# Thresholded attention with a SwiGLU layer: half-size input pieces, four chunks turned on TensorE, six weights buffers

## The chip, the cores and the metric

The kernel runs on one core of one Trainium2 chip. The metric is device time in microseconds, the median over several executions. Before the change it is 536.67 us over 4 runs (535.39 to 538.34). The profiled execution took 535.39 us, of which the span from its first to its last instruction is 533.6 us.

A core has five engines with queues of their own. TensorE (PE) multiplies matrices and writes to PSUM, VectorE (DVE) and ScalarE (ACT) work through rows, GpSimd (POOL) does the same on SBUF alone, and SyncE (SP) issues DMAs. Each queue runs in the order in which it was built; an instruction that waits holds back all that is behind it.

## The reference

q, k and v are [8 batches, 8 heads, 576 rows, 64] in float32. The attention keeps, in each row, only scores within tau = 0.02 of the row's maximum; the result goes through an RMS norm and a SwiGLU layer with 512 inputs and 1536 hidden units.

```python
scores = scale * np.matmul(q, k.transpose(0, 1, 3, 2))
thresh = np.max(scores, axis=-1, keepdims=True) - tau
scores = np.where(scores >= thresh, scores, -1000000000.0)
...
attn = np.exp(scores)
attn = attn / (np.sum(attn, axis=-1, keepdims=True) + 1e-09)
return np.matmul(attn, v)
...
xn = x / rms * rms_g
g = xn @ w_gate
silu = g * (1.0 / (1.0 + np.exp(-g)))
return (silu * (xn @ w_val)) @ w_out
```

## The kernel before

The 4608 output rows are worked on as 36 chunks of 128 rows. A batch has 576 rows, which is four chunks and a half; the halves of two batches make one chunk of its own ("v"), the others are "m". A chunk has four steps, one for each pair of heads, so there are 144 steps. A step is one row of scores for two heads:

- **Scores** (L690): TensorE multiplies q and k in float32 in two halves of PSUM, `s_ps`. The first 32 steps are made one at a time, the rest in bursts of 1024 columns, 1.78 steps each (L736).
- **Minima** (L723): VectorE writes -score/8 to `ssb` and keeps the row minimum `mx`. The second operand, which is added, is a row of zeros, `zrow` (L185).
- **Threshold and exponential**: GpSimd adds tau (L764), ScalarE masks with two Prelu operations (L775) and writes the exponential to one of three `wsb` buffers (L782).
- **Turning the weights**: for the first 16 steps TensorE transposes them (L827) and VectorE copies the result out (L836); from step 16 on, one DMA transpose for each step, issued by SP (L842), writes one of five `wt` buffers (NWT, L219).
- **Values product** (L860, L865): one for two steps, then VectorE divides by the sums (L882, L883).

After a chunk's four steps, `emit_x` squares the rows on ScalarE (L900), finds and applies the norm on GpSimd (L903 to L908) and turns the 128x512 rows `xn` into `xnT` by another DMA transpose on SP (L912). With `N_XPE` above 0 the first chunks would be turned by TensorE instead (L918 to L931); it is 0. Two or four chunks make a group for the **FFN**: 12 slices, each with a gate product (L966), a value product (L971), tanh on ScalarE, two VectorE operations (L983, L988), and then the output products (L1037, or L1012 for the last group).

**Inputs.** Batches 0 and 1 have loads of their own. From batch 2 on (`BLOCKED`), `emit_block_loads` brings the q and the k of two pairs of heads by one 576 KB DMA each (L369), GpSimd swaps 32-row blocks (L383) and VectorE turns 32x32 blocks (`emit_blocks`, L397 to L406). Values come in two 512 KB DMAs for each batch (L602), one for each half of the partitions, and GpSimd casts them for each pair of heads (L579). SP issues all of these loads, the transposes and the output stores through one queue.

**The order.** Nothing is ordered by hand. Every operation has a priority in steps, a modelled duration and what it depends on; `order_ops` (L56) plays them through and writes each engine's queue. `RANK` (L26) adds an offset for each kind of operation. For a DMA the planner adds an allowance until it has landed: `LAT_TR` for transposes, `LAT_QB`, `LAT_V` for the loads. A load is also tied to the score burst of the step that its priority names (`gated`, L249). So a changed allowance or rank moves instructions on all engines.

Of the kernel before, what the change touches and what calls it, by code (L numbers as in the profile page):

```python
# [25 lines left out]
RANK = dict(  # L26
    ACT={"emit_ffn/ev": 400, "emit_ffn/store": 40, "emit_ffn/tanh": -350, "emit_k_tail/ev": -230, "emit_q_tail/ev": -70, "emit_qk/ev": 390,
        "emit_softmax/prelu": 170, "emit_x/sq": -320},
    DVE={"emit_av/half": -39, "emit_blocks/turn_k": 90, "emit_blocks/turn_kt": 140, "emit_blocks/turn_q": 280, "emit_burst/ttr": -50, "emit_ffn/ev":
        185, "emit_ffn/gate": -20, "emit_ffn/silu": -44, "emit_k_tail/ev": -110, "emit_qk/ev": -120, "emit_softmax/ev": 250},  # L30
    PE={"emit_av/fn": -340, "emit_burst/fn": -110, "emit_ffn/gmm": 21, "emit_ffn/omm": 22, "emit_ffn/vmm": -20, "emit_k_tail/tr": 220,
        "emit_q_tail/tr": -70, "emit_softmax/tr": -110},
    POOL={"emit_block_loads/swap": 60, "emit_softmax/nthr": -240, "emit_x/mean": -110, "emit_x/norm": -50, "round_/<lambda>": 60, "main/<lambda>":
        760, "main/cast": -300},
)
# [114 lines left out]
def kernel(  # L150
# [12 lines left out]
    nc = tc.nc  # L163
# [20 lines left out]
    id16 = sb("id16", [128, 128], FP16)  # L184
    zrow = sb("zrow", [128, S], FP16)  # L185
    mhalf = sb("mhalf", [128, 1])
# [29 lines left out]
    esb = [sb(f"esb{i}", [128, S], FP16) for i in range(NES if set(WAYS) != {"pp"} else 0)]  # L216
    NW = 3
    wsb = [sb(f"wsb{i}", [128, 2, S], FP16) for i in range(NW)]
    NWT = 5  # L219
    wt = [sb(f"wt{i}", [128, 9, 128], FP16) for i in range(NWT)]  # L220
# [66 lines left out]
    def setup():  # L287
        o_id = add("POOL", 2000.0, -100, [], lambda o: make_identity(nc, id32))
        o_z = add("DVE", 350.0, -200, [], lambda o: nc.vector.memset(zrow, 0.0))

        def warm(o):

            for _ in range(WARM):
                nc.tensor.matmul(s_ps[0][:, 0:512], zrow[:, 0:128], zrow[:, 0:512], start=True, stop=True)

        o_w = add("PE", WARM * 380.0, -200, [o_z], warm)

        def consts(o):
            nc.vector.tensor_copy(out=id16, in_=id32)
            nc.vector.memset(mhalf, -0.5)  # L300

        def vconst(o):
            for i in range(2):
                nc.vector.memset(va[i][:, :, :, D:D + 1], 1.0)
                nc.vector.memset(va[i][64:128, :, 8], 0.0)
                nc.vector.memset(va[i][0:64, :, 9], 0.0)

        o_c = add("DVE", 300.0, -100, [o_id, o_z], consts)
        o_v = add("DVE", 2000.0, -90, [], vconst)
        o_g = add("SP", 350.0, -0.5, [], lambda o: nc.sync.dma_start(  # L310
            out=rmsg, in_=moe_rms_g.rearrange("(c p) -> p c", p=128)), dma=100.0)
        return o_id, o_c, o_v, o_g
# [46 lines left out]

    def emit_block_loads(b, g, prio):  # L360

        done = {}
        for j, src in ((1, k), (0, q)):
            before = turned[g, j] if (g, j) in turned else [x for t in tr_of for x in t[-NQK:]] + (tail_load["use", 0] if g else [])
            own = nat[:, g, 1 - j]

            def load(o, src=src, own=own):
                a0 = 2 * GROUP * g
                nc.sync.dma_start(out=own.rearrange("p a r d -> p a (r d)"),  # L369
                                  in_=src[b, a0:a0 + 2 * GROUP].rearrange("(a h) (m r) d -> h m a (r d)", h=2, r=RUN))  # L370

            pr = prio + BLOCK_STEP * (1 - j)
            lo = gated(add("SP", COST["sp_qb"], pr, before, load, dma=DMA_NS["qkb"], bulk=True), pr)
            lo.lat = LAT_QB
            done[j] = []
            for h in range(2):
                lower, upper = slice(64 * h, 64 * h + 32), slice(64 * h + 32, 64 * h + 64)
                moves = [(spare[upper], own[lower, :, :, 32:64]), (own[lower, :, :, 32:64], own[upper, :, :, 0:32]),
                         (own[upper, :, :, 0:32], spare[upper])]
                last = [lo] + spare_use[-1:]  # L380
                for dst, at in moves:
                    def swap(o, dst=dst, at=at):
                        nc.gpsimd.tensor_copy(out=dst, in_=at)  # L383

                    last = [add("POOL", COST["swap"], prio + SWAP_AT, last, swap)]
                spare_use.append(last[0])
                done[j] += last
            turned[g, j] = []
        return done

    def emit_blocks(b, p, prio, los):
# [18 lines left out]
        tq = gated(add("DVE", COST["turn_q"], prio, los[0] + free, turn_q), prio)  # L410
        turned[g, 0].append(tq)
        turned[g, 1] += [tk, tt]
        for c in range(4):
# [157 lines left out]
    def emit_v(b, prio):  # L571
# [13 lines left out]
        for p in range(NP):  # L585
# [12 lines left out]
            if b >= BLOCKED and p == 0:  # L598
                lo = []
                for g in range(2):  # L600
                    def load_block(o, g=g):
                        nc.sync.dma_start(out=vst8[64 * g:64 * g + 64].rearrange("m h (c d) -> m h c d", d=D),  # L602
                                          in_=v[b].rearrange("h (m r) d -> m h r d", r=RUN)[:, :, 4 * g:4 * g + 4])

                    pl = pr + V_FROM + V_STEP * g
                    lo.append(gated(add("SP", COST["sp_v"], pl, v_cast[-NP:], load_block, dma=2 * DMA_NS['v'], bulk=True), pl))
                    lo[-1].lat = LAT_V
            ca = add("POOL", COST["cast_v"], (pr + V_CAST if b >= BLOCKED else pr + 1 if b else p - 1.0), lo + free(p), round_(
                t[:, p, 0:8, 0:D].rearrange("q (c h) d -> q h c d", h=2),
# [18 lines left out]
    def emit_batch_inputs(b):  # L628
        base = first_step[b - 1] if b else -10
        if b == 1:  # L630
            base += B1_BASE
        if b < BLOCKED:
            emit_tail_load(b, base + (4 if b else 1))
        if b == 0:
            q0_use.extend(emit_first())
        else:
            for p in range(NP):
                pr = base + 3.3 * p + 3
                if b >= BLOCKED:
                    los = los if p % GROUP else emit_block_loads(b, p // GROUP, pr - 3)  # L640
                    emit_blocks(b, p, pr, los)
                else:
                    emit_qk(b, p, pr)
                if p == 0 and b < BLOCKED:
                    emit_k_tail(b, pr + 2)
        emit_v(b, base + 5 if b else -1)
        if b % 2 and b < BLOCKED:
            emit_q_tail(b // 2, v_step[b // 2] - 1.5)
# [27 lines left out]
    def emit_burst(segs, prio, runs):  # L676
# [35 lines left out]
        for s, lo, hi, at in segs:  # L712
# [7 lines left out]
            for h in range(2):  # L720
                def ttr(o, s=s, lo=lo, hi=hi, at=at, h=h, first=first, last=last):
                    m = s % 6
                    nc.vector.tensor_tensor_reduce(  # L723
                        out=ssb_of(s)[:, h, lo:hi], in0=s_ps[h][:, at:at + hi - lo], in1=zrow[:, lo:hi],
                        scale=-1.0 / 8.0, scalar=3.0e38 if first else mxp[m][:, h:h + 1], op0=ALU.add, op1=ALU.min,
# [33 lines left out]
    def emit_softmax(s):  # L759
# [80 lines left out]
        else:  # L840
# [5 lines left out]
            w_ready[s] = [t]  # L846

    def emit_av(s):

# [4 lines left out]
        def fn(o):  # L854
            for i in range(2):
# [14 lines left out]
        deps = w_ready[s - 1] + w_ready[s] + [x for bb in bs for i in range(2) for x in v_ready[bb, p1 - i]]  # L870
        o = add("PE", 2 * COST["av_main" if kind == "m" else "av_virt"], s + AV_PRIO, deps, fn, ring="R",
                mode=0 if kind == "m" else 3)
# [7 lines left out]
        def half(_):  # L880
# [5 lines left out]

        half_ev.append(add("DVE", COST["rz"] + COST["xmul"], s + HALF_PRIO, [o] + x_done.get(ci - 2, []), half,
                           frees=(o, 0)))

    def emit_x(ci, s, slot, off):  # L890
# [22 lines left out]

        a = add("DVE" if on_dve else "ACT", 660.0 if on_dve else COST["sq"], s + 1.5, half_ev[-2:] + xn_of[ci - 2:ci - 1], sq)
        bb = add("POOL", COST["pool_mean"], s, [a, o_c], mean)
        c = add("POOL", COST["xn"], s - 1, [bb], norm)
        x_done[ci] = [c]
        if ci < N_XPE:  # L918
# [4 lines left out]

            p_ = add("PE", 240.0, s, [c, o_c], trp, ring="R")
            xn_of.append(p_)
# [4 lines left out]

            return add("DVE", COST["evac_w"] + 50.0, s, [p_] + xnT_use.get(slot, []), ev, frees=(p_, 0))  # L931
        t = add("SP", COST["sp_tr"], s, [c] + xnT_use.get(slot, []), tr, dma=DMA_NS['xt'])
# [256 lines left out]
LAG = 8.0  # L1189
LAT_TR = 2500.0  # L1190
LAT_LD = 2000.0
# [18 lines left out]
WAYS = ("pp",)  # L1210
NSTAGE = 3
NQK = 3
BLOCKED = 2
BLOCK_STEP = 3.0
SWAP_AT = 4.0
V_STEP = 1.0
V_FROM = 6.0
V_CAST = 9.0
LAT_QB = 4500.0
LAT_V = 4000.0  # L1220
LAT_W = 3000.0
W_FROM = 2.0
W_STEP = 0.4
N_XPE = 0
N_PE = 16
# [40 lines left out]
```

## Time and profile before

| | |
|---|---|
| median of 4 runs | 536.67 us |
| profiled execution | 535.39 us |
| its span | 533.6 us |
| TensorE busy | 520.7 us |
| VectorE busy | 465.1 us |
| ScalarE busy | 444.0 us |
| GpSimd busy | 223.9 us |
| moved by DMA | 89.03 MB |

In the profile a busy share is the time in which at least one instruction of the engine runs. Matmuls overlap each other, and their ends are modelled. A row of the table of stretches reads: stretch, its length, the busy time (and instructions) of PE, PEld (the loading of the stationary operand, which overlaps PE), DVE, ACT and POOL, the granted TensorE clock, the mean busy share of the DMA engines, GB/s. A row of waits reads: who waited, for whom, microseconds in all, how often, the longest. A row of the timeline or the chain begins with its start and its length in microseconds. SPq is SP's issuing of a DMA. A DMA's "landing" runs from its issue to the arrival of its data, so the chain's DMA pieces are longer than SP's part of them.

The last score burst starts at about 455 us. Until then all parts run side by side; after it only the rest of the FFN is left, with TensorE busy for the whole of 460 to 520 us.

### The profile page before, as it was taken

Reading aid. Unit: us, or ns where it says so; the run is one execution under the profiler, and the core shown is the slowest. Engines: PE = TensorE matmul, PEld = TensorE weight load, DVE = VectorE, ACT = ScalarE, POOL = GpSimd, SP = SyncE. Lnnn points to the kernel's source line nnn. Section 1 sums busy time; section 2 is a strip of 40 time slices with the busy share of each in tenths; the row PEclk is TensorE's granted clock in tenths of the full one; section 3 lists DMA queues with packets and bytes.
Section 4 is the critical chain, followed back from the end, with each engine's and each line's share of the span. In section 5 each row is a group of like instructions: output and inputs, shape, how many; then the busy total and the mean of one; then the engine's idle time right before and its main releaser. Section 6 shows DMA issues by size and latency. Waiting matters only on the chain.

```text
span 533.6 us, 14315 instructions
## 1 busy us (share of the span) xinstructions
PE 520.7 (98%) x5352; PEld 273.7 (51%) x5352; DVE 465.1 (87%) x1342; ACT 444.0 (83%) x648; POOL 223.9 (42%) x478
## 2 busy tenths in 40 slices
PE   8999999999999999999999999999999999999995
PEld 4766676554645454445454454545454545444442
DVE  4998999978999999999999899989999888765641
ACT  5999999888997999889989999899999999831210
POOL 2368756615653157545743456445732022110000
PEclk9999999999999999999999999999999999999998
DMA  9999999959998789999997899999996768631103
GB/s 203 234 298 307 193 200 187 211 84 227 202 178 142 165 162 176 200 200 183 192 180 153 168 192 207 186 211 175 210 165 120 143 119 118 137 66 30 30 22 98
DMA packets 220486, 89.03 MB, mean 167 GB/s; under 512 B 196864, under 2 KB 206592, under 8 KB 220416
## 3 DMA queue, kind: packets, MB, share of 16 engines
q1 hardware_dynamic: 217616, 86.02, 81.7%
q0 software_dynamic: 1600, 1.57, 1.9%
q8 instruction: 42, 0.69, 0.6%
q10 hardware_dynamic: 1200, 0.52, 0.4%
q14 instruction: 28, 0.23, 0.1%
HBM read 37.75 MB, written 9.44 MB: 88 GB/s over the span
## 4 chain that ended last, share of the span: by engine, by line
PE 66%; DVE 15%; DMA 7%; ACT 6%; issue 3%; POOL 1%; SPq 1%; DVEq 0%; ACTq 0%; POOLq 0%
PE s_ps L690 20%; PE ring L966 12%; PE ring L971 12%; PE ring L1037 11%; DVE ssb L723 8%; DMA wt<-wsb 4%; PE ring L865 4%; ACT ssb L775 3%; DMA xnT<-xn 2%; PE s_ps L1012 2%; DVE sl L983 2%; ACT wsb L782 2%; PE ring L860 1%; DVE hf L988 1%; DVE stg L988 1%
## 5 line engine op out<-in xcount | busy, mean ns | idle before, releaser
L775 ACT ACTIVATE ssb<-ssb,nth 128x576 f32<-128x576 f32 x288 | 209.8, 766 | 16.6 <-POOL nth L764 15.8
L723 DVE CUSTOM_DVE_ANT_0 ssb<-s_ps,zrow 128x576 f32<-128x576 f32 (+8 forms) x288 | 169.3, 635 | 8.9 <-PE s_ps L690 6.8
L690 PE MATMUL s_ps<-qkt 64*64 64x288 f32 (+9 forms) x2256 | 171.2, 411 | 1.5 <-DVE mx L723 0.8
L782 ACT ACTIVATE wsb<-ssb 128x1152 f16<-128x1152 f32 x144 | 166.8, 1159 | 4.2 <-DMA wt<-wsb 1.9
L690 PEld LDWEIGHTS s_ps<-qkt 64*64 64x64 f32 (+1 forms) x2256 | 81.2, 134 | 67.4 <-issue 25.9
L966 PE MATMUL ring<-xnT,wg 128*128 128x512 f16 (+1 forms) x456 | 107.1, 357 | 2.0 <-DMA xnT<-xn 1.5
L971 PE MATMUL ring<-xnT,wv 128*128 128x512 f16 (+1 forms) x456 | 107.0, 357 | 0.1
L980 ACT ACTIVATE th<-ring 128x512 f32<-128x512 f32 (+1 forms) x114 | 61.6, 541 | 39.2 <-PE ring L966 38.8
L764 POOL TENSOR_SCALAR nth<-mx 128x2 f32<-128x2 f32 x144 | 30.8, 214 | 148.4 <-DVE mx L723 141.8
L983 DVE SCALAR_TENSOR_TENSOR sl<-th,ring 128x512 f32<-128x512 f32 (+1 forms) x114 | 70.7, 622 | 9.5 <-ACT th L980 9.4
L966 PEld LDWEIGHTS <-wg 128*128 128x128 f16 x480 | 43.3, 98 | 53.2 <-issue 15.3
L971 PEld LDWEIGHTS <-wv 128*128 128x128 f16 x480 | 44.1, 98 | 48.2 <-issue 9.0
L723 DVE CUSTOM_DVE_ANT_0 ssb<-s_ps,zrow,mxp 128x128 f32<-128x128 f32 (+7 forms) x112 | 52.9, 509 | 15.6 <-PE s_ps L690 13.1
L865 PE MATMUL ring<-va,wt 128*128 128x65 f16 (+1 forms) x1280 | 51.7, 193 | 0.0
L865 PEld LDWEIGHTS <-wt 128*128 128x128 f16 (+1 forms) x1280 | 46.3, 100 | 4.3
L1037 PE MATMUL ring<-wo,hf 128*128 128x512 f16 x204 | 48.0, 379 | 0.0
L988 DVE TENSOR_TENSOR stg<-ring,sl 128x512 f16<-128x512 f32 (+1 forms) x59 | 36.7, 627 | 2.2
L1037 PE MATMUL ring<-wo,stg 128*128 128x512 f16 x156 | 36.8, 379 | 0.0
L988 DVE TENSOR_TENSOR hf<-ring,sl 128x512 f16<-128x512 f32 (+1 forms) x55 | 34.0, 623 | 1.6
L903 POOL TENSOR_SCALAR irm<-ssq 128x1 f32<-128x1 f32 x36 | 6.9, 190 | 66.4 <-ACT xn L900 65.6
L383 POOL COPY spare<-qkx 32x576 f32<-32x576 f32 x48 | 31.6, 658 | 7.1 <-DMA qkx<-in_k_dram 2.8
L860 PE MATMUL ring<-va,wt 128*128 128x130 f16 (+1 forms) x160 | 32.3, 225 | 1.4 <-DMA wt<-wsb 1.4
(71 smaller groups left out, 495.0 us busy)
## 6 DMA issues: line engine op xcount, KB each, us to landing
qkx<-in_k_dram SPq DMA_DIRECT2D x12, 576.0 KB, 4.7
qkx<-in_q_dram SPq DMA_DIRECT2D x12, 576.0 KB, 4.7
out_dram<-osb SPq DMA_DIRECT2D x51, 128.0 KB, 2.6
vst<-in_v_dram SPq DMA_DIRECT2D x12, 512.0 KB, 5.5
stg<-in_moe_w_gate_dram SPq DMA_DIRECT2D x6, 512.0 KB, 5.8
stg<-in_moe_w_val_dram SPq DMA_DIRECT2D x6, 512.0 KB, 6.1
vst<-in_v_dram SPq DMA_DIRECT2D x8, 256.0 KB, 4.3
wt<-wsb SPq DMA_TRANSPOSE x128, 3.7
```

Of the source, the lines that this page charges most:

```text
L690: nc.tensor.matmul(s_ps[h][rows, at:at + hi - lo], lhs(hs), k_of(bb, p, h)[hs, lo:hi], start=True, stop=True)
L723: nc.vector.tensor_tensor_reduce(out=ssb_of(s)[:, h, lo:hi], in0=s_ps[h][:, at:at + hi - lo], in1=zrow[:, lo:hi], scale=-1.0 / 8.0, scalar ...
L775: nc.scalar.activation(out=sb_[:, h], in_=sb_[:, h], func=PRELU, scale=-1.0, bias=nth[m][:, h:h + 1], **PRELU_KW)
L782: nc.scalar.activation(out=wsb[s % NW], in_=sb_, func=AF.Exp)
L860: nc.tensor.matmul(ring[o.slot[0]][rs, at:at + 2 * (D + 1)], w[:, 4, rs], va[vi][:, p, 8:10].rearrange("p e d -> p (e d)"), start=True, st ...
L865: nc.tensor.matmul(ring[o.slot[0]][rs, at:at + D + 1], w[:, 5 * h + j, rs], va[vi][:, p, 2 * j + h], start=False, stop=(h == 1 and j == 3))
L966: nc.tensor.matmul(ring[o.slot[0]][:, 0:n], wg[d][:, fs], xnT[slot][:, d, 0:n], start=(d == 0), stop=(d == 3))
L971: nc.tensor.matmul(ring[o.slot[0]][:, 0:n], wv[d][:, fs], xnT[slot][:, d, 0:n], start=(d == 0), stop=(d == 3))
L980: nc.scalar.activation(out=th[i][:, 0:n], in_=ring[g.slot[0]][:, 0:n], func=AF.Tanh, scale=0.5)
L983: nc.vector.scalar_tensor_tensor(out=sl[i][:, 0:n], in0=th[i][:, 0:n], scalar=1.0, in1=ring[g.slot[0]][:, 0:n], op0=ALU.add, op1=ALU.mult)
L988: nc.vector.tensor_tensor(out=hf[hi][:, 0:n], in0=ring[vv.slot[0]][:, 0:n], in1=sl[i][:, 0:n], op=ALU.mult)
L1037: nc.tensor.matmul(ring[(first or o).slot[0]], hf[hs[fc][0]][:, 128 * j:128 * (j + 1)], wo[:, fc], start=(fc == 0), stop=(fc == NFC - 1))
```

## The change

It has five parts.

1. The 576 KB loads of q and k become two of 288 KB, each for one pair of heads, at 1.25-step distances (`LOAD_STEP`) from the beginning of the batch before; a piece waits for the turns of its own pair only. The two 512 KB values loads become four of 256 KB for half of the heads each (`V_PARTS`), and a cast waits for the two pieces of its own heads. The planner's allowances for them go down by 500 ns.
2. `N_XPE` = 4: the rows of the first four chunks are turned by four 128x128 TensorE transposes and one VectorE copy.
3. Six `wt` buffers instead of five, and `LAT_TR` goes from 2500 to 3000 ns. To make room, the row of zeros gives way to a single column that is broadcast; the warm-up matmuls read the first `xn` buffer, cleared for that.
4. Other ranks in all four tables.
5. `soon`, an offset for the first chunks, is added to some priorities. It is set to 0 and does nothing.

```diff
-    PE={"emit_av/fn": -340, "emit_burst/fn": -110, "emit_ffn/gmm": 21, "emit_ffn/omm": 22, "emit_ffn/vmm": -20, "emit_k_tail/tr": 220,
-        "emit_q_tail/tr": -70, "emit_softmax/tr": -110},
+    PE={"emit_av/fn": -370, "emit_burst/fn": 16, "emit_ffn/gmm": 20, "emit_ffn/omm": 23, "emit_ffn/vmm": -40, "emit_k_tail/tr": 210, "emit_q_tail/tr":
+        -160, "emit_qk/tr": 60, "emit_softmax/tr": -40, "emit_x/trp": 20},
...
-    zrow = sb("zrow", [128, S], FP16)
+    zcol = sb("zcol", [128, 1], FP16)
...
-    NWT = 5
+    NWT = N_WT
...
+        def zero(o):
+            nc.vector.memset(zcol, 0.0)
+            nc.vector.memset(xn[0], 0.0)
...
-            def load(o, src=src, own=own):
-                a0 = 2 * GROUP * g
-                nc.sync.dma_start(out=own.rearrange("p a r d -> p a (r d)"),
-                                  in_=src[b, a0:a0 + 2 * GROUP].rearrange("(a h) (m r) d -> h m a (r d)", h=2, r=RUN))
-
-            pr = prio + BLOCK_STEP * (1 - j)
+            for a in range(GROUP):
+                p = GROUP * g + a
...
+                def load(o, src=src, own=own, a=a, p=p):
+                    nc.sync.dma_start(out=own[:, a].rearrange("p r d -> p (r d)"),
+                                      in_=src[b, 2 * p:2 * p + 2].rearrange("h (m r) d -> h m (r d)", r=RUN))
+
+                pr = base + LOAD_STEP * (GROUP * (2 * g + 1 - j) + a)
...
-                last = [lo] + spare_use[-1:]
+                last = los + spare_use[-1:]
...
+                for i in range(2 * V_PARTS):
+                    g, hs = i % 2, slice(i // 2 * H // V_PARTS, (i // 2 + 1) * H // V_PARTS)
...
-                        out=ssb_of(s)[:, h, lo:hi], in0=s_ps[h][:, at:at + hi - lo], in1=zrow[:, lo:hi],
+                        out=ssb_of(s)[:, h, lo:hi], in0=s_ps[h][:, at:at + hi - lo], in1=zcol.to_broadcast([128, hi - lo]),
...
-LAT_TR = 2500.0
+LAT_TR = 3000.0
...
+N_W = 3
+N_WT = 6
...
-BLOCK_STEP = 3.0
+LOAD_STEP = 1.25
+V_PARTS = 2
...
-LAT_QB = 4500.0
-LAT_V = 4000.0
+LAT_QB = 4000.0
+LAT_V = 3500.0
...
-N_XPE = 0
+N_XPE = 4
+SOON = (0, 0.0)
```

## The prediction

> **What bounds the kernel now.** I read the page's busy shares first, then the table of stretches, then who waited for whom on TensorE, then the chain and SP's timeline around each of those waits.
>
> ```profile
> span 533.6 us, 14315 instructions
> PE 520.7 (98%) x5352; PEld 273.7 (51%) x5352; DVE 465.1 (87%) x1342; ACT 444.0 (83%) x648; POOL 223.9 (42%) x478
> ...
> 20.00:60.00 40.00, 37.97 (x507) 27.21 (x506) 37.05 (x106) 37.89 (x55) 29.45 (x57) 1.00 1.09 280
> 60.00:100.00 40.00, 39.88 (x487) 26.24 (x481) 38.36 (x112) 39.54 (x65) 23.53 (x46) 1.00 1.06 197
> 100.00:280.00 180.00, 177.44 (x1917) 90.36 (x1916) 170.48 (x515) 164.62 (x234) 90.29 (x191) 1.00 0.94 177
> 280.00:460.00 180.00, 178.90 (x1945) 88.36 (x1945) 167.96 (x518) 169.14 (x239) 72.93 (x164) 1.00 0.88 166
> ```
>
> TensorE is idle for 533.6 - 520.7 = 12.9 us. The stretches place it: 1.7 us before 20, 2.0 in 20 to 60, 0.1 in 60 to 100, 2.6 in 100 to 280, 1.1 in 280 to 460, and 5.4 behind the last matmul. From 60 to 460 only 3.8 us are left to take. Matmul ends are modelled, so a little more is hidden: in the timeline eight 65-column matmuls take 0.41 us though one is shown with 193 ns, so they start about 31 ns apart and each pause behind them is shown up to 0.2 us short. The granted clock is 1.00 in every stretch to 460, so it takes no part.
>
> ```profile
> PE ring L966 <- DMA xnT<-xn: 1.5, 2, 0.9
> PE ring L860 <- DMA wt<-wsb: 1.4, 3, 0.8
> ```
>
> Five waits, 2.9 us, are for DMA transposes: twice for rows of xn (L912), three times for softmax weights (L842). With 0.2 us hidden at each, **3.9 us** hang on late transposes. SP's timeline shows what stands in front of three of them, and the chain what it made of them:
>
> ```profile
> 92.55 0.69 SPq L602 DMA_DIRECT2D vst<-in_v_dram  x1
> 94.30 2.04 SPq L842 DMA_TRANSPOSE wt<-wsb  x1
> ...
> 94.30 7.49 DMA wt<-wsb
> ...
> 118.13 0.57 SPq L369 DMA_DIRECT2D qkx<-in_k_dram  x1
> 118.80 1.19 SPq L912 DMA_TRANSPOSE xnT<-xn  x1
> ...
> 118.80 4.80 DMA xnT<-xn
> ...
> 273.28 0.68 SPq L602 DMA_DIRECT2D vst<-in_v_dram  x1
> 274.35 1.21 SPq L912 DMA_TRANSPOSE xnT<-xn  x1
> ...
> 274.35 6.17 DMA xnT<-xn
> ...
> DMA to landing us min/median/max: 3.2/3.7/7.5
> ```
>
> Each late transpose was issued right behind a 512 or 576 KB load; the last line is the weights transposes' usual time to landing, 3.7 us.
>
> **The change, part by part.**
>
> *Half-size pieces.* From the third batch on, 24 q and k loads become 48 and 12 values loads become 24, with the same bytes and the same runs in each row. A load that is met halfway has half as much left to move. SP pays 36 more issues: 24 x 0.59 us (L369) + 12 x 0.68 us (L602) = 22 us. Cover: SP waited 134.9 + 37.8 us for ACT at its weights transposes, so it has time; without that cover each issue would delay the transposes queued behind it by 0.6 us. In the built order 34 places before have a transpose as the next instruction behind a load; after, there are 50, and 11 of 59 places still hold two or three pieces side by side.
>
> [...] The rows: 512 KB of values land in 5.5 us, 256 KB in 4.3 us, 64 KB in 3.2 us. [...] I follow the rows, because what is won is not the load's own time but that of a transpose behind it. Bounds: -3.9 us (all five waits gone) to +1.8 us (late transposes grow with the places, 3.9 x 50/34 = 5.7).
>
> *Margin for transposes (2500 to 3000 ns), six weights buffers.* The planner puts each use of a transpose 0.5 us later. Counted in the built order, the TensorE work between the scores of a pair of steps and its values product grows by about 0.5 us on average from step 16 on, and the smallest distance from 9.1 to 10.1 us; the pair that was late at 100.8 us (steps 30 and 31) goes from 9.1 to 11.1. The first FFN matmul of a group after its last values product: third group unchanged at 8.8 us, sixth 10.1 to 11.3. So at least the third group's wait may stay, unless the half loads shorten it. The sixth buffer buys nothing by itself: no weights transpose waited for a values product in the list of waits, only for ACT. Its use is to pay for the longer distance. I take **-3.9 us** for these two parts together, the upper end, since two independent means meet at four of the five places.
>
> *Rows of the first four chunks by TensorE.* Added: 16 transposes and four 128x512 copies on VectorE; removed: four DMA transposes (1.23 us of SP each, 3.3 us to landing), on which nobody is shown waiting. TensorE: nine such transposes take 0.67 us in the timeline, so four take 0.30 and all 1.2 us. [...] VectorE: the 128x512 copy at L836 takes 0.415 us, 1.7 us in all, beside 2.95 us of idle time in 20 to 60 and 1.6 in 60 to 100. New wait: TensorE's transposes need GpSimd's normalised rows. Before, the rows were ready 4.5, 4.9, 6.9 and 4.7 us after the values product (26.0 to 30.5, 37.9 to 42.8, 49.5 to 56.4, 61.7 to 66.4 us). In the new order the first set stands where before's timeline had about 31.0, the second at about 43.4: 0.5 us after. Behind a waiting set stand the next weights transposes and the next score burst, for which VectorE waits. Bounds 0 to +4 us (1 us each); nearest is the 0.5 us to spare, so I take +0.3, and of the 1.2 us I let 0.4 vanish in the idle time of 20 to 60: **+1.1 us**.
>
> *A [128,1] zero column broadcast* instead of a row, read by all 400 score minima. Nearest row: L883 reads a broadcast operand, 425 ns for 256 columns, against 420 and 409 for L988's two forms of that size without one. 0 to 16 ns; at 16 ns it is 400 x 16 = 6.4 us of VectorE, of which under half could show on TensorE (+3). I take 0. Clearing the first xn buffer for the warm-up replaces clearing a row: 0.
>
> *Other ranks.* The number of score bursts (96) and of changes between score and other matmuls (190) is the same. What moves: FFN matmuls left behind the last burst fall from 322 to 284, so 38 x 216 ns = 8.2 us of them come earlier. In the tail TensorE is 100% busy, so this wins only what fills idle time: 3.8 - 2.9 = 0.9 us. **-1.0 us**, with 0 and -3 (hidden pauses at bursts) as bounds. The values' casts wait for the two pieces that they read, swaps for both halves as before, and a half load for one pair's turns instead of two: nothing later than before.
>
> Sum: -3.9 + 1.1 - 1.0 = -3.8 us on a profiled execution of 535.39 us (span 533.6, 1.8 us around it). That execution is the fastest of the four shown; applied to their median, 536.67 - 3.8 = **532.9 us**, 0.7% less.
>
> **Rivals.**
> *Same time.* The transposes stay late at group heads (third group's distance unchanged), half of the 3.9 us stays, the freed rest pays for the turned rows: -1.9 + 1.1 - 0.5 = -1.3, 535.4 us. For: DMA share near 1 with or without halves. Against: every late transpose has a big load right ahead of it.
> *Slower: SP's single queue.* A half costs a transpose as much as a whole load, and there are 50 such meetings instead of 34: +1.8, plus 0.6 us of issue on each meeting; if one in six of the 16 new ones comes late by its issue time, +1.6; with the turned rows +1.1: 541.2 us. It decides once the transposes' median landing plus their wait on SP exceeds today's by the 0.5 us of added margin. For: SP already holds back transposes behind issues of 1.3 us. Against: SP waits for ACT, not ACT for SP, at all but two exponentials (1.9 us).
> *VectorE pays for the broadcast:* -3.8 + 3.0 = -0.8, 535.9 us.
> That the moves take no effect is excluded: the built order has them all.
>
> **How the numbers follow.** Forecast 0.50, same time 0.15, broadcast 0.05, slower 0.30. Its own range is 528 to 534: at best -3.9 - 3.0 with the turned rows wholly in idle time, 529.8, less half of the spread of the runs shown (1.5). The range over the cases is 528 to 541.2, leaving the far end of the slower case out. Half a per cent, 2.7 us, is about what a measurement of this kernel tells from no change. Faster 0.50, within 0.20, slower 0.30.
>
> **What would show it.** Right: the two rows of TensorE's waits for transposes at under 1 us together; the weights transposes' longest landing under 6 us; about 61 us of TensorE work behind the last score burst; the score minima of 576 columns still at about 752 ns; the four new sets without a wait for GpSimd. Wrong: longer waits at L860 and L966's successors, a landing median above 4.2 us, VectorE's minima longer by 10 ns or more, or TensorE idle in 60 to 460 above 4 us.

## The result, and the profile after

The changed kernel takes **535.09 us** (median of 34 runs, 533.44 to 536.5), the kernel before 536.88 (55 runs, 534.3 to 539.66). The ratio is 0.9965, with an interval from 0.9955 to 0.9974: about 1.8 us less, where 3.8 were forecast. The direction and the place of the gain were as predicted, its size just under half.

The page of the changed kernel, and its stretches (columns as before: stretch, length, PE, PEld, DVE, ACT, POOL, clock, DMA share, GB/s):

```profile
span 532.6 us, 14403 instructions
PE 520.1 (98%) x5368; PEld 274.4 (52%) x5368; DVE 465.5 (87%) x1347; ACT 443.8 (83%) x648; POOL 223.9 (42%) x478
```

```profile
0.00:20.00 20.00, 16.87 (x160) 9.42 (x161) 11.76 (x37) 13.20 (x25) 4.85 (x16) 1.00 0.93 192
20.00:60.00 40.00, 37.96 (x510) 27.03 (x511) 37.41 (x108) 38.16 (x57) 28.85 (x55) 1.00 1.09 292
60.00:100.00 40.00, 39.83 (x503) 26.52 (x496) 38.47 (x112) 39.60 (x65) 25.34 (x50) 1.00 0.95 168
100.00:280.00 180.00, 179.12 (x1925) 91.74 (x1923) 170.52 (x516) 164.34 (x234) 88.87 (x188) 1.00 0.93 178
280.00:460.00 180.00, 179.26 (x1899) 88.54 (x1898) 166.99 (x507) 164.68 (x234) 72.52 (x162) 1.00 0.87 162
```

TensorE's idle time from 60 to 460 falls from 3.8 to 0.17 + 0.88 + 0.74 = 1.8 us. The span falls by only 1.0, because this execution lost 1.4 us more in its first 20 us (16.87 busy, before 18.32). That is scatter of the start: the kernels below that have the same first 20 us show 16.9 to 18.4 there. So the two spans aren't compared below; the medians and the stretch from 60 to 460 are.

Who waited for whom on TensorE (microseconds in all, times, longest), after:

```profile
PE ring L870 <- DMA wt<-wsb: 0.5, 1, 0.5
PE ring L976 <- DVE sl L993: 0.5, 1, 0.5
PE ring L981 <- DVE sl L993: 0.2, 1, 0.2
```

Of the five waits for DMA transposes, 2.9 us in all, one of 0.5 us is left; the row for xnT is gone. In the next two rows an FFN product waits for VectorE's SiLU step, which empties a PSUM slot. Before, one such wait of 0.4 us was shown, for another VectorE operation.

The weights transposes by their line, then the score minima of 576 columns (busy us, mean ns, idle before):

```profile
DMA to landing us min/median/max: 3.2/3.6/5.9
```

```profile
L730 DVE CUSTOM_DVE_ANT_0 ssb<-s_ps,zcol 128x576 f32<-128x576 f32 x176 | 126.0, 752 | 6.1 <-PE s_ps L697 5.3 <-POOL nth L771 0.3
```

The longest landing falls from 7.5 to 5.9 us with the median as it was: only the late ones have gone. The minima take 752 ns, as they did with a row of zeros, so the broadcast costs nothing.

Pauses between matmuls can also be worked out from their start times: start to start, less what the columns take (0.215 us for 512: four of them stand with 0.86 us on the changed kernel's chain). From 60 to 460 us they are 2.7 us less after. The pauses of 0.2 us or more, by what ended them:

| | before | after |
|---|---|---|
| a late DMA transpose | 4.0 us in 6 | 0.7 us in 1 |
| other waits ahead of FFN or values products | 0.8 us in 2 | 2.4 us in 7 |
| of these, a wait for VectorE | 0.5 us | 2.1 us |
| score matmuls | 0.75 us in 3 | none |

The sixth late transpose, 0.3 us at 228 us, was too short for the list of before. The last score burst now ends at 463.7 us (before 456.6), and behind it 63.3 us of TensorE work are left (before 71.5).

### The profile page after: what moved, and what is told of

It reads as the page before. It is cut to its first block, busy times and chain, and to the rows that moved or that the text cites. A ratio compares the mean times of both kernels' runs of the same rounds, so it can differ in the third digit from the quotient of the medians.

```text
span 532.6 us, 14403 instructions
## 1 busy us (share of the span) xinstructions
PE 520.1 (98%) x5368; PEld 274.4 (52%) x5368; DVE 465.5 (87%) x1347; ACT 443.8 (83%) x648; POOL 223.9 (42%) x478
## 4 chain that ended last, share of the span: by engine, by line
PE 69%; DVE 11%; ACT 8%; DMA 4%; issue 4%; POOL 2%; SPq 1%; DVEq 0%; POOLq 0%; ACTq 0%
PE s_ps L697 21%; PE ring L1047 13%; PE ring L981 12%; PE ring L976 12%; DVE ssb L730 7%; PE ring L875 4%; ACT ssb L782 4%; PE s_ps L1022 2%; ACT wsb L789 2%; DMA qkx<-in_q_dram 2%; DVE sl L993 1%; PE ring L870 1%; ACT th L990 1%; DMA wt<-wsb 1%; PE s_ps L1047 1%
## 5 line engine op out<-in xcount | busy, mean ns | idle before, releaser
L730 DVE CUSTOM_DVE_ANT_0 ssb<-s_ps,zcol 128x576 f32<-128x576 f32 (+8 forms) x288 | 169.5, 636 | 6.1 <-PE s_ps L697 5.3
L697 PE MATMUL s_ps<-qkt 64*64 64x288 f32 (+8 forms) x2256 | 170.0, 411 | 0.8 <-DVE mx L730 0.8
L697 PEld LDWEIGHTS s_ps<-qkt 64*64 64x64 f32 x2256 | 81.7, 134 | 65.1 <-issue 28.5
L976 PE MATMUL ring<-xnT,wg 128*128 128x512 f16 (+1 forms) x464 | 109.2, 358 | 0.6 <-DVE sl L993 0.5
L981 PE MATMUL ring<-xnT,wv 128*128 128x512 f16 (+1 forms) x456 | 106.9, 357 | 0.5 <-DVE sl L993 0.2
L993 DVE SCALAR_TENSOR_TENSOR sl<-th,ring 128x512 f32<-128x512 f32 (+1 forms) x116 | 72.0, 623 | 11.3 <-ACT th L990 11.1
L981 PEld LDWEIGHTS <-wv 128*128 128x128 f16 x480 | 44.6, 98 | 50.1 <-issue 10.9
L976 PEld LDWEIGHTS <-wg 128*128 128x128 f16 x480 | 43.0, 98 | 52.6 <-issue 15.1
L730 DVE CUSTOM_DVE_ANT_0 ssb<-s_ps,zcol,mxp 128x128 f32<-128x128 f32 (+7 forms) x112 | 52.9, 510 | 13.3 <-PE s_ps L697 13.2
L998 DVE TENSOR_TENSOR stg<-ring,sl 128x512 f16<-128x512 f32 (+1 forms) x57 | 35.5, 628 | 2.4
L998 DVE TENSOR_TENSOR hf<-ring,sl 128x512 f16<-128x512 f32 (+1 forms) x57 | 35.5, 627 | 1.8
L893 DVE TENSOR_TENSOR xsb<-ring,rz 128x256 f32<-128x256 f32 x72 | 30.6, 425 | 3.5
L1047 PEld LDWEIGHTS <-hf 128*128 128x128 f16 x216 | 20.0, 98 | 25.8 <-issue 3.5
```

The lines of the kernel that those rows point to most:

```text
L697: nc.tensor.matmul(s_ps[h][rows, at:at + hi - lo], lhs(hs), k_of(bb, p, h)[hs, lo:hi], start=True, stop=True)
L730: nc.vector.tensor_tensor_reduce(out=ssb_of(s)[:, h, lo:hi], in0=s_ps[h][:, at:at + hi - lo], in1=zcol.to_broadcast([128, hi - lo]), scale ...
L976: nc.tensor.matmul(ring[o.slot[0]][:, 0:n], wg[d][:, fs], xnT[slot][:, d, 0:n], start=(d == 0), stop=(d == 3))
L981: nc.tensor.matmul(ring[o.slot[0]][:, 0:n], wv[d][:, fs], xnT[slot][:, d, 0:n], start=(d == 0), stop=(d == 3))
L993: nc.vector.scalar_tensor_tensor(out=sl[i][:, 0:n], in0=th[i][:, 0:n], scalar=1.0, in1=ring[g.slot[0]][:, 0:n], op0=ALU.add, op1=ALU.mult)
L998: nc.vector.tensor_tensor(out=hf[hi][:, 0:n], in0=ring[vv.slot[0]][:, 0:n], in1=sl[i][:, 0:n], op=ALU.mult)
```

## Experiments: the pieces

In the five kernels here, and in those on the turned rows, the planner saw nothing of the edit, so each engine's queue stands as in the kernel that was edited, but for the instructions named. The ratios are all to the kernel before, to runs of it made beside each kernel (their medians are 536.2 to 537.6 us), so they differ a little from a ratio to 536.88; 0.001 is 0.54 us.

**Before's order, each large load cut into two halves issued back to back.**

```diff
+                for a in range(GROUP):
+                    nc.sync.dma_start(out=own[:, a]..., in_=src[b, a0 + 2 * a:a0 + 2 * a + 2]...)
...
+                        for hs in (slice(0, H // 2), slice(H // 2, H)):
+                            nc.sync.dma_start(out=vst8[64 * g:64 * g + 64, hs]..., in_=v[b, hs]...)
```

> The kernel before with its order kept, but each 576 KB q or k load and each 512 KB values load issued as two halves, one directly behind the other. Theory (it is the spreading over the steps that helps, not the size, since the same bytes still stand in front of a transpose): within 0.5 us of before, the waits for transposes stay at about 2.9 us. Rival (size alone): they fall below 1.5 us and the time falls by 1.5 us. Third (each further DMA costs its issue and its fixed part in front of a transpose): 1 to 2 us slower.

Measured: 536.42 us, 0.998 [0.9966, 0.9995]. TensorE's waits for transposes in it:

```profile
PE ring L862 <- DMA wt<-wsb: 1.6, 2, 1.2
...
PE ring L968 <- DMA xnT<-xn: 0.7, 1, 0.7
```

They come to 2.3 us in three waits, against 2.9 in five. Cutting alone is worth about 1 us by the ratio (0.3 to 1.8 by its interval), and 36 more issues on SP cost nothing that shows. Where that 1 us comes from the trace doesn't show: by start times the pauses at late transposes are 3.9 us in seven, as good as before's 4.0 in six. It is no cure in this order: the transpose that was late at 100.8 us still lands after 6.16 us (before 7.49), and the longest landing of a weights transpose is 7.9 us.

**The changed order, q and k whole** (576 KB, at the place of the second half).

```diff
+                    if a:
+                        nc.sync.dma_start(out=own..., in_=src[b, 2 * p - 2:2 * p + 2]...)
```

> The changed kernel with its order kept, but each pair of 288 KB q or k pieces is one 576 KB load at the second piece's place. Theory (half pieces matter because a transpose behind a whole load lands late): waits of TensorE for transposes return, 1 to 2.5 us together, longest landing of the weights transposes back over 7 us, time 1 to 2 us over the changed kernel (ratio 0.998 to 1.0). Rival (only the planner's longer distance counts): no wait returns, within 0.4 us of the changed kernel, ratio 0.9965.

Measured: 534.85 us, 0.9958 [0.9942, 0.9975], no different from the change itself. By start times the pauses at late transposes rise to 1.7 us in four, but in this order the halves of q and k bring nothing that the times show.

**The changed order, values whole too** (as above, and 512 KB at each of the first two of the values' four places).

```diff
+                        if i < 2:
+                            nc.sync.dma_start(out=vst8[64 * g:64 * g + 64]..., in_=v[b]...)
```

> The changed kernel with its order kept and no half pieces at all: q and k whole at the second piece's place, values whole (512 KB) at the places of the first two of four pieces. Theory (the order keeps transposes and their uses far enough apart, the size of the loads in front does not matter): within 0.5 us of the changed kernel, ratio 0.995 to 0.998, waits for transposes under 1.2 us. Rival (two of the three late transposes shown before stood behind 512 KB of values, so the values' halves are what helps): waits for transposes 2 us or more, ratio 0.999 or more.

Measured: 540.64 us, 1.0083 [1.0065, 1.01]. That overturned the reading of the run before, that halves don't matter in the changed order. One row of its waits is enough to see what it hit:

```profile
PE ring L872 <- DMA wt<-wsb: 4.6, 5, 1.6
```

It left open whether the values do it by themselves, and whether by the size of a piece or by their places. The next two bear on this.

**The changed order, values whole, q and k in halves** (the second edit alone).

> The changed kernel in its own order; q and k stay in halves, only the values come whole: 512 KB at each of the first two of their four places. If a weights transpose comes late because a 512 KB values load is right ahead of it in SP's queue, this alone repeats the loss seen with all loads whole: 540 to 541 us, ratio 1.007 to 1.009, waits for wt of 3 to 5 us, longest landing of wt above 7 us. If the loss needs whole q and k as well (too many bytes in flight at once), it is 535 to 537 us, ratio 0.996 to 1.000.

Measured: 539.99 us, 1.0069 [1.005, 1.0089], so the values alone cost (1.0069 - 0.9965) x 537 = 5.6 us. SP's timeline around one of the late transposes:

```profile
334.63 0.67 SPq L610 DMA_DIRECT2D vst<-in_v_dram  x1
335.42 2.39 SPq L850 DMA_TRANSPOSE wt<-wsb  x1
337.91 1.56 SPq L923 DMA_TRANSPOSE xnT<-xn  x1
339.57 1.41 SPq L850 DMA_TRANSPOSE wt<-wsb  x1
341.03 0.65 SPq L610 DMA_DIRECT2D vst<-in_v_dram  x1
```

The chain of waits in the same stretch (start, length, what):

```profile
335.42 6.14 DMA wt<-wsb
341.55 0.02 issue
341.57 0.02 ACTq L790
341.59 0.04 issue
341.64 1.16 ACT wsb L790
342.80 0.30 ACT ssb L783
343.10 6.48 DMA wt<-wsb
```

The transpose is issued 0.8 us behind a 512 KB load and takes 6.14 us to land, where 3.6 is usual. ScalarE waits for it too: there are three `wsb` buffers, and the next exponential can't be written until one has been turned. So one late transpose makes the next exponential late, and the transpose of that one, issued behind the second 512 KB load and two output stores, takes 6.48 us again. The list shows only 2.8 us in five waits for transposes; by start times they are 4.2 us in seven, 3.5 more than in the changed kernel, and the pauses at FFN and values products behind VectorE grow by 1.2 (3.3 against 2.1). Together that is 4.7 of the 5.0 us between the two profiled spans (537.6 and 532.6), whose first 20 us are alike. The same place in the changed kernel:

```profile
333.21 0.67 SPq L609 DMA_DIRECT2D vst<-in_v_dram  x1
334.00 2.02 SPq L849 DMA_TRANSPOSE wt<-wsb  x1
```

Behind 256 KB the same transpose lands after 4.61 us and is nowhere on the chain. Values of 256 KB land in 4.0 us (median), of 512 KB in 5.6.

**The same places, each 512 KB as two halves back to back.**

```diff
+                            for hs in (slice(0, H // 2), slice(H // 2, H)):
+                                nc.sync.dma_start(out=vst8[64 * g:64 * g + 64, hs]..., in_=v[b, hs]...)
```

> As the kernel with whole values, but each 512 KB is issued as two halves back to back at the same two places. If the size of one DMA holds up the transpose behind it, halves help even side by side: 535 to 536.5 us, ratio 0.9965 to 0.999, longest landing of wt near 6 us. If the bytes ahead of the transpose count, it is as with whole values, 540 to 541 us (ratio 1.007 to 1.009): then it is the spreading over four places, not the cutting, that the change gains by.

Measured: 536.26 us, 0.999 [0.9972, 1.0007]. With the same bytes at the same places, 4.2 us of the 5.6 come back by cutting alone (3.7 by the two medians). The two transposes on the chain above land after 4.95 and 5.24 us instead of 6.14 and 6.48, and the longest landing falls from 7.1 to 5.7 us. So in this order it is mostly the size of one DMA that costs the time. That spreading over four places brings the remaining 1.3 us isn't shown: the intervals of this kernel and the change overlap. Nor is it seen where the 4.2 us were saved. The trace is that of the slowest of this kernel's 12 runs (537.88 us), and in it TensorE still waits:

```profile
PE ring L872 <- DMA wt<-wsb: 3.3, 3, 2.1
```

That these waits are shorter in the other runs is argued from the shorter landings. In the order of before, as the first of these kernels shows, the same cut did less.

## Experiments: the turned rows

**The four turned sets done twice** (the same result written twice, everything else in place).

```diff
-                for d in range(4):
+                for d in 2 * list(range(4)):
...
+                for _ in range(2):
                     nc.vector.tensor_copy(out=xnT[slot]..., in_=ring[p_.slot[0]]...)
```

> The changed kernel with the four turned row sets done twice (16 more TensorE transposes, four more VectorE copies, same order of everything else). Theory (the turned rows cost their work, 1.1 us, because TensorE is the bound): 1.0 to 1.3 us over the changed kernel, so about 0.7 us under the kernel before (ratio 0.9987). Rival (they lie in TensorE's pauses and cost nothing; the gain fell short elsewhere): the same as the changed kernel, ratio 0.9965.

Measured: 536.19 us, 0.9987 [0.9971, 1.0003]: 1.2 us more than the change, about what four sets were predicted to cost (1.1). The two intervals overlap slightly.

**The same four sets by DMA transposes, at the same places.**

```diff
-                for d in range(4):
-                    nc.tensor.transpose(ring[o.slot[0]]..., xn[ci % 2]..., id16)
+                tr(o)
...
-                nc.vector.tensor_copy(out=xnT[slot]..., in_=ring[p_.slot[0]]...)
+                pass
```

> The changed kernel with its order kept, but the rows of the first four chunks turned by a DMA transpose each, issued at the place where TensorE had turned them; the 16 TensorE transposes and four VectorE copies are gone. Theory: 1.0 to 1.3 us under the changed kernel, ratio to before about 0.9942. Rival (free in the pauses): the same as the changed kernel. A second rival (DMA transposes of the first chunks would have come late behind loads): slower than the changed kernel by up to 2 us, with TensorE waits for xnT before 75 us.

Measured: 542.29 us, 1.0096 [1.0073, 1.0118], 7 us more than the change. It has one long wait of its own, and the chain runs through it:

```profile
PE ring L973 <- DMA xnT<-xn: 4.4, 1, 4.4
```

```profile
45.03 0.69 POOL xn L918
45.72 0.03 issue
45.75 6.04 DMA xnT<-xn
51.79 0.04 issue
51.83 1.01 PE ring L973 x4
```

The first FFN product stands 4.4 us too early for a row that comes by DMA. And 4.4 us don't account for 7. The rest is in the column of the granted clock (the DMA column adds up the times of packets, so it can pass 1):

```profile
48.00:50.00 2.00, 0.00 (x0) 0.00 (x0) 0.84 (x3) 1.23 (x2) 1.96 (x3) 1.00 1.65 210
50.00:52.00 2.00, 0.17 (x2) 0.10 (x2) 0.00 (x0) 0.00 (x0) 1.57 (x3) 0.69 0.80 166
52.00:54.00 2.00, 2.00 (x12) 1.22 (x14) 0.70 (x3) 1.09 (x3) 0.00 (x0) 0.50 1.07 384
54.00:56.00 2.00, 2.00 (x19) 0.74 (x12) 0.40 (x3) 1.79 (x2) 0.00 (x0) 0.50 1.16 239
56.00:58.00 2.00, 2.00 (x17) 1.63 (x14) 1.83 (x5) 0.22 (x1) 0.39 (x2) 0.60 1.13 341
58.00:60.00 2.00, 2.00 (x35) 1.27 (x34) 1.62 (x4) 1.97 (x4) 1.19 (x2) 1.00 1.04 404
...
20.00:60.00 40.00, 32.78 (x408) 22.70 (x405) 30.25 (x84) 31.59 (x46) 23.22 (x44) 0.91 1.11 284
```

TensorE stands still from 47.4 to 51.8 us. At about 50.8 us the granted clock falls to 0.50, and it stays so until about 57.6. Work runs in it from 51.8 on: 16 score matmuls of 288 columns take 2.20 us, where the same number took 1.20 at a clock of 1.00. Taken as half speed, these 5.8 us cost an estimated 2.9. In the stretch from 20 to 60 us TensorE is idle for 5.2 us more than in the changed kernel (32.78 us busy against 37.96), and 1.1 us of turning is gone: 5.2 + 2.9 - 1.1 = 7.0.

**Only the first two chunks turned by TensorE**, the other two by DMA at the same places.

```diff
+                if ci > 1:
+                    return tr(o)
```

> The changed kernel with its order kept, rows of chunks 0 and 1 turned by TensorE and of chunks 2 and 3 by DMA transposes at the same places; the first use of those is some 7 us later. Theory (turning costs 0.3 us of TensorE for each chunk, and only the first group needs it): 0.5 to 0.6 us under the changed kernel, ratio 0.9955. Rival (a DMA transpose is late here too, as the second chunk's was): a wait for xnT of 1 us or more before 80 us, and slower than the changed kernel.

Measured: 535.07 us, 0.9977 [0.9963, 0.9991]. No wait for xnT appears, so two of the four sets could as well have come by DMA. The 0.6 us that leaving them out should save doesn't show, but that is no more than these intervals can tell.

**The same with q and k whole**, both free edits in one.

> The changed kernel in its own order with both single edits that cost nothing put together: q and k in whole 576 KB loads at the place of the second half, and only the first two chunks turned by TensorE. If their effects add up, 0.6 us of TensorE work is saved and nothing is lost: 534 to 535 us, ratio 0.994 to 0.997. If a whole q or k load makes one of the two DMA transposes late that replace the turned sets, 536 to 538 us, ratio 0.998 to 1.002, with a wait for xnT on TensorE of 1 us or more.

Measured: 534.69 us, 0.9971 [0.9956, 0.9986]. That is the change's own time again; none of these kernels is clearly faster. Its longest landing of a weights transpose is 7.0 us, with no loss of time: a late landing costs only where something waits for it.

## Experiments: the planner

In these the planner laid out the whole kernel anew, so every queue moves.

**The kernel before with margin 3000 ns, six weights buffers and the zero column.**

```diff
-    NWT = 5
+    NWT = 6
...
-LAT_TR = 2500.0
+LAT_TR = 3000.0
```

> The kernel before planned anew with the new allowance (3000 ns), six weights buffers and the zero column that makes room for them; whole loads, old ranks, rows by DMA transposes. Theory (distance alone removes the late transposes): waits for transposes fall from 2.9 us to under 1 us, ratio 0.994 to 0.996, no turned rows to pay for. Rival (a changed allowance with ranks that were not fitted to it reshuffles the order and brings as many new waits): ratio 0.998 to 1.004.

Measured: 543.46 us, 1.0101 [1.0074, 1.0128].

```profile
PE ring L865 <- DMA wt<-wsb: 3.2, 4, 1.3
...
PE ring L971 <- DMA xnT<-xn: 1.3, 2, 0.9
```

Although 500 ns more are allowed for each transpose, more of them are late: 4.5 us in six waits against 2.9 in five.

**The changed kernel with margin 2500 ns.** Only `LAT_TR` goes back.

> The changed kernel planned anew with the old allowance for transposes, 2500 ns. Theory (the longer distance between transpose and use is what removed the late transposes, since whole q and k loads in the kept order brought them back by only 0.4 us): TensorE waits for transposes rise from 0.5 us to 2 us or more, time 1.5 to 2.5 us over the changed kernel, ratio 0.9995 or so. Rival (ranks and the other parts carry it): waits stay under 1 us, ratio 0.996 to 0.997.

Measured: 541.59 us, 1.0077 [1.0052, 1.0102].

```profile
PE s_ps L697 <- DVE mxp L730: 3.2, 3, 2.7
...
PE ring L976 <- DMA xnT<-xn: 1.8, 2, 1.0
```

**The changed kernel without turned rows.** `N_XPE` goes back to 0.

> The changed kernel planned anew with no chunk turned by TensorE (rows of all chunks by DMA transposes, the planner knowing of them). Theory (the turned rows cost their TensorE work, 0.8 to 1.1 us by the doubled run, and buy only an earlier first FFN slice): about 1 us under the changed kernel, ratio 0.9945, first gate product later than in the changed kernel. Rival (the earlier start of the FFN fills TensorE before 100 us and is worth more than 1.1 us): slower than the changed kernel, ratio 0.998 or more, and more FFN work left behind the last score burst.

Measured: 544.51 us, 1.0124 [1.009, 1.0158].

```profile
PE s_ps L697 <- DVE mxp L730: 4.7, 3, 2.4
```

**The changed kernel with before's ranks, and before with the new ranks.** The four rank tables change places.

> The changed kernel planned anew with the ranks of before. Theory (the parts pay only in an order that the ranks were fitted to): 3 us or more over before, ratio 1.006 or more, with single waits of TensorE over 1 us. Rival (the parts carry the gain, the ranks add little): ratio 0.995 to 0.999.

> The kernel before planned anew with the new ranks and nothing else. Theory (fitted ranks and parts belong together): ratio 1.005 or more. Rival (the new ranks alone make the better order, and move FFN work ahead of the last burst as in the changed kernel): ratio 0.995 to 0.999.

Measured: 540.15 us, 1.0073 [1.0053, 1.0093], and 542.41 us, 1.0122 [1.0096, 1.0149]. One row of each:

```profile
PE s_ps L697 <- DVE mxp L730: 3.4, 4, 1.6
...
PE s_ps L690 <- DVE mxp L723: 4.1, 4, 2.7
```

**The changed kernel nudged.** One spacing of the FFN, which is no part of the change, goes from 16.0 to 16.1.

```diff
-PACE = 16.0
+PACE = 16.1
```

> The changed kernel planned anew with one number moved that means nothing by itself: the FFN's pace from 16.0 to 16.1 steps for a group. It shows how far the time scatters when only the order is reshuffled. If the order is robust: within 0.3 us of the changed kernel, ratio 0.996 to 0.997. If the ranks are fitted to one order: 1 us or more away, nearly always up, ratio 0.998 or more.

Measured: 537.45 us, 0.9986 [0.9964, 1.0008].

```profile
PE ring L870 <- DMA wt<-wsb: 2.6, 3, 1.5
```

A nudge that means nothing brings 2.6 us of late transposes back, with all five parts of the change in place, and takes more than half of the gain away. Its interval reaches down to the change's own ratio, so the size of that loss is uncertain. Here lies the limit of all six. The other five are 4 to 7 us slower than the kernel before. In the four with other margin, no turned rows or exchanged ranks the score bursts wait 3.2 to 4.7 us for VectorE's minima so far (`mxp`), a wait that neither kernel's list shows. Three of them also run for about 3.4 us at half clock, by the granted clock of three 2 us stretches in each: 0.75, 0.50 and 0.89 from 124 us on without turned rows, 0.77, 0.50 and 0.88 from 130 us on in the changed kernel with before's ranks, 0.65, 0.50 and 1.00 from 130 us on in before with the new ones. Taken as half speed, that is an estimated 1.7 us each. It seems that ranks, margin and turned rows fit one order of the queues. What any one part is worth in time these runs don't show.

## Why the prediction was half right

- **Late transposes, -3.9.** Measured: 4.0 us of pauses before, 0.7 after, so -3.3; where all waits were to go, one of 0.7 us for a weights transpose is there at 289.9 us. The mechanism held in part: in the changed order whole values ahead of transposes cost 5.6 us, and cutting them there brings most of it back; in before's order cutting alone left 3.9 us of such pauses. "Each late transpose" was too much said: it holds for the three that the prediction shows, while those issued at 307.5 and 334.3 us stood behind another transpose and behind two output stores. Of the two means that were costed together, the pieces are shown to act, and of the pieces the values' only; of the margin it is shown only that with six buffers, in before's order laid out anew, it doesn't cure.
- **Halves against whole loads.** Cutting all loads into two halves back to back gained about 1 us in before's order, with 36 more issues on SP. Cutting the values alone brought 4.2 us in the changed order, with the DMA engines at a mean share of 0.93 and 0.87 (the changed kernel's long stretches). The rows of landing times were the right thing to go by.
- **Turned rows, +1.1.** Doubling them costs 1.2 us, in line; halving them showed no saving. No wait for GpSimd's rows appeared, so the +0.3 within the sum for that was not needed.
- **Zero column, 0.** Right: 752 ns for 576 columns both times.
- **Other ranks, -1.0: this term failed.** The work did move: 376 matmuls stood behind the last score burst before, 338 after, the 38 predicted. But it did not fill idle time. The prediction let it fill all of the 0.9 us that would be left once the transposes' waits were gone, and put nothing for waits that the moved work itself would meet. Instead 1.8 us of idle time are left from 60 to 460: FFN and values products now stand where VectorE hasn't yet done what they wait for (the rows for L976 and L981 above). Pauses of 0.2 us or more ahead of them grow from 0.8 to 2.4 us, +1.6, while those at score matmuls fall by 0.75. The term measures about +0.9 instead of -1.0.

How firmly do these pauses belong to the ranks? They are no accident of one execution: in the eight other traces in the changed kernel's order, those behind VectorE come to 1.9 to 3.3 us. And they go with the ranks wherever the planner laid out an order. With the new ranks, in five orders, they are 1.7 to 4.2 us, with 310 to 346 matmuls behind the last burst; with the old, in three orders, 0.5 to 1.4 us, with 376 to 406. Exchanging nothing but the ranks moves both: before with the new ranks has 1.7 us and 346 matmuls (0.5 and 376 without), the changed kernel with the old ranks 1.0 us and 406 (2.1 and 338). As every queue moved in these exchanges, this is a strong hint and no proof.

Sum by these: -3.3 + 1.1 + 0.9 = -1.3, against 1.8 less in the medians. So most of the 2.0 us that were forecast too many hang on the ranks' term, and about 0.6 on the transposes'.

Of the rivals, SP's single queue did not decide: there are 50 meetings of load and transpose instead of 34, but with shorter loads. The same-time case came nearest in size (-1.3), by luck: it let half the late transposes stay, and nearly all went.

All five marks of being right came true: waits for transposes under 1 us (0.5), longest landing of weights transposes under 6 us (5.9), about 61 us of TensorE work behind the last score burst (63.3), minima at 752 ns, no wait for GpSimd at the turned rows. None of them could show that the moved work finds no idle time to fill. The sign of being wrong that might have, idle time from 60 to 460 above 4 us, was set too high: it was 3.8 in the kernel before already.

## What to carry over

Where transposes share a queue with large loads, look at what is issued right ahead of each late one, and try cutting that load, even if the DMA engines are busy (a mean share of 0.87 and 0.93 here): a load that TensorE doesn't wait for set the time of a transpose behind it (6.14 us to landing behind 512 KB, 4.61 behind 256). How much it brings depends on the order (4.2 us in one, about 1 in the other). Count work that is moved forward as a gain only after finding the idle time it fills and the buffer slot it needs there. And in a kernel laid out by a planner, test a part with the order held fixed; laid out anew, one small nudge took away about half of the gain under study.

## What was not expected of the hardware

In these runs a stall could cost more than its length, and its length alone didn't tell whether it would. Half clock followed the 4.4 us wait above, for 6.8 us, but also pauses of only 1.7 us (in the changed kernel with before's ranks), 2.2 and 2.6 us (in before with the new ranks and in the changed kernel without turned rows), for about 3.4 us each. A pause of 2.9 us in the changed kernel with margin 2500 ns left the clock at 1.00. These are the stretches around the pauses of 1.7 us and of 2.9 us, the first five rows from the changed kernel with before's ranks, the others from the one with margin 2500 ns:

```profile
126.00:128.00 2.00, 1.80 (x30) 0.80 (x22) 0.74 (x3) 1.93 (x3) 1.82 (x4) 1.00 0.92 241
128.00:130.00 2.00, 0.35 (x6) 0.22 (x6) 2.00 (x9) 0.90 (x2) 1.65 (x4) 1.00 1.05 226
130.00:132.00 2.00, 2.00 (x30) 1.12 (x30) 1.97 (x6) 2.00 (x4) 1.70 (x4) 0.77 1.09 198
132.00:134.00 2.00, 2.00 (x9) 0.59 (x5) 1.39 (x8) 0.28 (x1) 0.86 (x3) 0.50 0.59 176
134.00:136.00 2.00, 2.00 (x25) 1.20 (x23) 2.00 (x8) 1.50 (x3) 1.53 (x4) 0.88 0.97 183
...
120.00:122.00 2.00, 0.61 (x8) 0.24 (x4) 1.25 (x6) 1.97 (x4) 1.45 (x4) 1.00 0.87 201
122.00:124.00 2.00, 0.66 (x7) 0.43 (x10) 1.56 (x8) 1.82 (x4) 0.41 (x2) 1.00 1.05 258
124.00:126.00 2.00, 2.00 (x46) 1.65 (x39) 0.29 (x1) 2.00 (x3) 0.00 (x0) 1.00 1.12 242
126.00:128.00 2.00, 1.18 (x14) 0.58 (x12) 2.00 (x7) 1.97 (x4) 0.21 (x1) 1.00 1.13 201
```

In the first, TensorE is busy for 0.35 us of the 2 us from 128 to 130, and the granted clock is below 1.00 from the next stretch on. In the second it is busy for 1.27 us of the 4 us from 120 to 124, and every stretch after is granted 1.00, as far as 136 us. What decides between the two is not shown; no run was made to test it.
